# Another written-out order for a convolution and feed-forward kernel: the transposing DMAs of h get a larger latency in the plan

## The chip, the cores and the metric

The kernel runs on one core of a Trainium2 chip. The metric is the device time of one execution in microseconds, the median of nine runs. A core has five engines that each follow an instruction queue of their own in order: the matrix engine (PE), the vector engine (DVE), the scalar engine (ACT), GpSimd (POOL) and SP, which here does nothing but issue DMAs. An instruction waits on semaphores for what it needs from other queues, and everything behind it in its queue waits with it.

## The reference

Four layers work on x of 2048 rows by 512 columns in bfloat16: a gated long convolution, a SwiGLU feed-forward layer, and the same two again with the same weights.

```python
def _A_ref(q, k, v, shift_k, ssm_k, ssm_D):
    # k_shift: a causal filter of 4 taps per column over k
    kv = k_shift * v
    # y[s] = sum over t <= s of ssm_k[:, s - t] * kv[t], by FFTs of length 2 * 2048
    y = y + kv * ssm_D[None, None, :]
    return q * y

def _B_ref(x, w_gate, w_up, w_down):
    g = _silu(x @ w_gate)
    u = x @ w_up
    return (g * u) @ w_down

x = A_q
x = x + _A_ref(_layernorm(x, axis=-1), A_k, A_v, A_shift_k, A_ssm_k, A_ssm_D)
x = x + _B_ref(_layernorm(x, axis=-1), B_w_gate, B_w_up, B_w_down)
x = x + _A_ref(_layernorm(x, axis=-1), A_k, A_v, A_shift_k, A_ssm_k, A_ssm_D)
x = x + _B_ref(_layernorm(x, axis=-1), B_w_gate, B_w_up, B_w_down)
return x
```

The convolution's inputs k, v and ssm_k are the same in both layers, so its result y is computed once and used twice.

## The kernel before

**Tiling.** The 2048 positions are cut into four blocks of 512, and a block into four rows (r = 0 to 3) of 128 positions, one on each partition. The long convolution is done block by block with short Fourier transforms. For block b the filter's values h (the tile `hn`, loaded with columns on the partitions) are turned so that positions lie on the partitions (`hs`), transformed by matmuls with a table (`fwd`), moved out of PSUM by ACT and combined by additions on DVE (`H`, `G`). The same is done with k times v (`vt`, `X`). Products of the spectra are added up in `Z` on DVE (L641 to L655), and matmuls with `inv` give the block of y (`Yk`).

**Turning h.** For blocks 0 and 1, h is transposed on PE (L465). For blocks 2 and 3 `transpose_h_dma` does it (L575 to L585): four copies on ACT (L579) bring `hn` into `hr`, one for each 128 columns, and then SP issues four transposing DMAs (L583), one for each row r, from `hr` to `hs`. A row needs all four copies. The matmuls `ps<-hs,fwd` (L299) use one row each, two per row.

**Feed-forward layer.** It works in units of 256 positions (layer, block c, half h). `prologue` normalises the rows, multiplies with y, adds to x (`xc`), normalises again into `z`, and an SP transposing DMA turns each `z` into `zT` (L831). `ffn` then goes through 14 column blocks of 128 in groups of 4, 4, 4 and 2. Eight matmuls of 256 columns fill one PSUM bank with two blocks of the gate or of the up product (`pf`, L299), ACT applies SiLU (L900, `sg`) or casts (L904, `ht`), DVE multiplies them (L907), and the `pd` matmuls with `wd_sb` (L920) take the product down. The result is added to x by ACT and DVE (L946 to L959), or by a matmul with the identity (L879). PSUM banks come in three rings: `pf` (4), `pd` (2) and `pc` (2).

**What sets the order.** All work is first recorded as a list of operations by `add`, each with its engine, a cost and, for DMAs, a latency. `ORDER` is a table written out in the source with one rank for each of the 1564 operations. `Plan.order` sorts the operations by rank, walks through them with the costs and latencies to choose which buffer of its ring each tile takes, and `Plan.issue` emits them. The instructions of one engine follow each other in that order. Costs and latencies don't move any instruction when `ORDER` is given. They only take part in the choice of buffers, and in the number of warm-up matmuls (L1159) that fill gaps at the start.

**The start.** POOL makes the constants `m` (L974), `eps` (L972), `fq` (L976) and the identity, DVE makes phases from them (L1012, L1016), and ACT makes the Fourier table from the phases by a sine (L1018). DVE clears `drow` (L973), SP loads one row into it (L1003), and DVE adds it to row 0 of h (L478). SP's first nine loads are h, k, the taps, drow, v and x of block 0, h and v of block 1, and the gate weights; two transposing DMAs then turn `fwd` into `inv` (L1069). k of block 0 is transposed on PE (L354, `pt<-ident,kn`), and its taps are applied by matmuls `ps<-dg,kTb`. The first block's y goes straight into the first unit: `m` (L729), `ps<-m,inv` (L735), `n` and `xc` (L837 to L842), `z` (L802), a transpose of z on PE (L854, `ptz`) and two copies into `zT` (L857, L859), after which the first `pf` matmul can run.

Of the kernel before, what the change touches and what calls it, by code (L numbers as in the profile page):

```python
# [48 lines left out]
ORDER = [4, 0, 1, 8, 3, 5, 6, 2, 7, 11, 15, 17, 22, 13, 14, 12, 10, 16, 19, 23, 20, 18, 21, 24, 29, 26, 36, 27, 32, 37, 31, 43, 25, 39, 28, 33, 30,  # L49
         34, 56, 76, 66, 71, 52, 59, 48, 75, 35, 42, 41, 53, 57, 62, 67, 69, 65, 50, 46, 60, 55, 9, 38, 45, 40, 49, 51, 54, 44, 64, 81, 47, 108, 143,  # L50
         148, 154, 63, 70, 77, 78, 83, 73, 74, 80, 82, 87, 84, 89, 90, 93, 96, 61, 68, 85, 88, 92, 86, 79, 91, 98, 94, 103, 105, 121, 127, 135, 173,
         100, 102, 95, 101, 106, 97, 104, 109, 99, 112, 58, 72, 107, 115, 110, 117, 123, 126, 116, 119, 124, 113, 125, 129, 122, 128, 132, 130, 133,
         139, 145, 147, 153, 138, 140, 149, 111, 114, 120, 118, 131, 134, 144, 141, 137, 146, 163, 165, 160, 156, 168, 171, 136, 142, 155, 161, 151,
         157, 162, 170, 158, 166, 152, 177, 198, 200, 167, 188, 194, 207, 174, 181, 172, 150, 178, 179, 191, 218, 164, 185, 176, 190, 175, 180, 182,
         183, 186, 189, 227, 232, 195, 203, 192, 241, 212, 187, 196, 193, 201, 202, 197, 208, 205, 209, 211, 215, 221, 224, 230, 219, 222, 229, 225,
         235, 239, 242, 248, 251, 255, 266, 268, 269, 275, 280, 284, 287, 294, 291, 295, 298, 300, 306, 308, 313, 315, 319, 233, 238, 245, 250, 254,
         247, 262, 257, 199, 206, 216, 204, 217, 223, 169, 184, 213, 214, 220, 226, 270, 277, 282, 285, 293, 303, 234, 237, 243, 279, 288, 292, 231,
         260, 310, 317, 321, 325, 343, 328, 335, 331, 159, 332, 323, 336, 276, 267, 299, 314, 338, 346, 353, 360, 383, 390, 395, 402, 405, 409, 416,
         423, 429, 444, 441, 434, 458, 492, 473, 477, 484, 495, 457, 466, 470, 489, 501, 514, 527, 536, 210, 228, 240, 256, 258, 263, 244, 252, 236,
         246, 273, 302, 283, 253, 264, 249, 259, 261, 272, 278, 286, 307, 316, 311, 271, 301, 289, 297, 274, 290, 296, 304, 309, 320, 324, 305, 312,  # L60
         265, 281, 318, 322, 327, 326, 330, 347, 352, 342, 349, 339, 350, 329, 340, 355, 363, 380, 333, 345, 356, 364, 361, 368, 354, 370, 379, 392,
         396, 371, 384, 367, 373, 375, 382, 351, 366, 387, 404, 400, 385, 394, 388, 397, 401, 406, 403, 408, 410, 413, 334, 337, 341, 344, 348, 357,
         358, 359, 362, 365, 369, 372, 376, 374, 377, 378, 381, 386, 389, 393, 391, 398, 426, 432, 420, 433, 437, 440, 448, 450, 452, 455, 461, 467,
         464, 468, 469, 472, 485, 491, 480, 482, 422, 425, 407, 415, 424, 428, 411, 417, 438, 462, 475, 414, 419, 451, 471, 418, 430, 436, 460, 476,
         488, 493, 446, 454, 431, 439, 427, 445, 465, 474, 481, 500, 497, 479, 487, 443, 490, 494, 503, 506, 524, 516, 551, 622, 675, 399, 435, 447,
         456, 478, 483, 486, 509, 499, 510, 512, 521, 523, 518, 525, 533, 537, 548, 559, 546, 550, 496, 507, 504, 532, 535, 543, 557, 555, 560, 564,
         568, 583, 570, 579, 588, 592, 613, 617, 600, 604, 412, 421, 449, 442, 453, 459, 498, 502, 554, 558, 566, 571, 505, 534, 545, 549, 553, 565,
         575, 578, 539, 541, 526, 530, 590, 584, 603, 606, 595, 597, 609, 616, 585, 625, 593, 463, 601, 589, 581, 610, 632, 620, 596, 634, 608, 615,
         643, 640, 633, 645, 654, 660, 666, 680, 670, 687, 709, 698, 702, 713, 717, 692, 695, 699, 710, 731, 736, 724, 727, 719, 722, 725, 732, 741,
         745, 761, 751, 757, 754, 708, 626, 684, 734, 629, 624, 637, 649, 662, 672, 678, 682, 766, 773, 778, 781, 786, 791, 801, 811, 822, 817, 848,  # L70
         845, 864, 859, 855, 863, 874, 881, 858, 872, 877, 916, 869, 875, 886, 899, 915, 927, 937, 934, 946, 952, 964, 960, 973, 986, 513, 519, 511,
         515, 517, 522, 508, 538, 542, 572, 586, 540, 573, 556, 563, 531, 552, 528, 544, 576, 614, 598, 520, 529, 567, 574, 562, 569, 547, 561, 580,
         623, 628, 577, 587, 591, 599, 621, 641, 644, 661, 651, 676, 679, 691, 631, 639, 594, 605, 611, 618, 619, 630, 642, 671, 664, 648, 653, 582,
         612, 635, 647, 602, 636, 658, 677, 674, 659, 665, 638, 655, 646, 650, 652, 657, 668, 681, 685, 656, 663, 607, 627, 669, 683, 688, 686, 690,
         693, 667, 673, 689, 697, 706, 715, 694, 704, 723, 755, 733, 714, 729, 720, 749, 737, 743, 701, 712, 763, 769, 772, 759, 765, 747, 752, 750,
         762, 726, 738, 770, 777, 775, 764, 774, 742, 748, 776, 780, 779, 784, 782, 790, 700, 705, 696, 703, 707, 711, 716, 718, 721, 728, 730, 739,
         735, 740, 744, 746, 753, 756, 760, 758, 767, 795, 799, 797, 800, 806, 809, 816, 820, 819, 826, 829, 834, 838, 832, 837, 839, 843, 851, 860,
         865, 853, 857, 813, 802, 783, 788, 798, 804, 792, 796, 789, 793, 808, 835, 824, 794, 805, 803, 810, 821, 830, 818, 823, 841, 850, 846, 787,
         812, 814, 825, 807, 815, 842, 847, 852, 861, 866, 828, 856, 831, 836, 862, 873, 871, 876, 892, 888, 910, 771, 768, 785, 827, 833, 844, 849,
         868, 880, 890, 896, 904, 909, 906, 912, 914, 917, 926, 945, 949, 938, 943, 882, 895, 854, 894, 913, 923, 951, 965, 953, 969, 978, 989, 985,  # L80
         993, 995, 1007, 1011, 1014, 1025, 1029, 1027, 1034, 867, 870, 840, 878, 903, 883, 891, 898, 954, 959, 961, 975, 974, 977, 931, 956, 966,
         970, 925, 930, 919, 921, 939, 941, 982, 991, 996, 1004, 999, 1002, 1018, 1012, 1031, 1060, 972, 1064, 1038, 1000, 1054, 983, 1026, 1020,
         924, 1033, 1057, 1081, 1045, 1078, 1066, 1075, 1088, 1096, 1108, 1114, 1101, 1133, 1138, 1139, 1143, 1140, 1145, 1165, 1170, 1163, 1168,
         1147, 1150, 1151, 1154, 1174, 1179, 1156, 1158, 1183, 1188, 1201, 1193, 1196, 1198, 1061, 1030, 1035, 1040, 1056, 1062, 1051, 1094, 1141,
         1210, 1205, 1226, 1231, 1240, 1236, 1243, 1248, 1253, 1258, 1263, 1273, 1265, 1267, 1268, 1272, 1275, 1278, 1289, 1305, 1288, 1291, 893,
         900, 879, 885, 902, 907, 884, 889, 922, 935, 944, 911, 929, 887, 901, 920, 933, 897, 908, 942, 955, 962, 928, 947, 932, 936, 905, 918, 940,
         950, 957, 971, 988, 958, 963, 948, 968, 981, 998, 1008, 1013, 1021, 1044, 1050, 1048, 967, 979, 976, 987, 980, 997, 990, 1006, 1009, 1019,
         1039, 994, 1003, 1005, 1017, 1001, 1015, 984, 992, 1022, 1036, 1042, 1032, 1041, 1028, 1037, 1010, 1043, 1016, 1024, 1047, 1063, 1055, 1046,
         1053, 1023, 1049, 1059, 1067, 1065, 1070, 1068, 1073, 1120, 1083, 1072, 1077, 1058, 1071, 1076, 1089, 1079, 1091, 1100, 1121, 1115, 1052,
         1085, 1099, 1106, 1084, 1092, 1103, 1110, 1113, 1127, 1132, 1112, 1119, 1090, 1098, 1095, 1104, 1069, 1074, 1125, 1135, 1144, 1109, 1117,  # L90
         1128, 1134, 1136, 1142, 1148, 1146, 1153, 1080, 1086, 1082, 1087, 1093, 1097, 1105, 1102, 1107, 1111, 1116, 1122, 1118, 1123, 1124, 1126,
         1130, 1137, 1129, 1131, 1149, 1159, 1155, 1160, 1161, 1164, 1171, 1172, 1175, 1178, 1186, 1182, 1189, 1197, 1192, 1200, 1204, 1217, 1225,
         1215, 1218, 1169, 1177, 1152, 1162, 1167, 1173, 1157, 1166, 1181, 1191, 1207, 1199, 1206, 1194, 1208, 1180, 1190, 1184, 1212, 1219, 1224,
         1232, 1176, 1185, 1203, 1209, 1187, 1195, 1211, 1216, 1222, 1229, 1238, 1214, 1223, 1221, 1227, 1230, 1235, 1241, 1254, 1262, 1270, 1360,
# [141 lines left out]
def kernel(  # L236
# [18 lines left out]
    KD, NF = D // P, F // P  # L255
# [319 lines left out]
    def transpose_h_dma(b):  # L575
        hr = new("s8", "hr", [P, R, KD, P], parts=KD)
        hs = new("hs", "hs", [P, R, D], parts=R)
        for dt in range(KD):
            add("ACT", 0.565, lambda dt=dt: nc.scalar.copy(  # L579
                out=hr.t[:, :, dt], in_=hn[b].t[:, dt, :].rearrange("d (p r) -> d r p", r=R)), r=[hn[b]], w=[(hr, (dt,))],  # L580
                conv=True)
# [611 lines left out]
```

## Time and profile before

| | |
|---|---|
| median of nine runs | 347.36 us (346.83 to 349.63) |
| profiled execution | 347.36 us |
| its span, first to last instruction | 345.6 us |
| granted clock of PE | 1.00 |
| PE busy | 336.7 us, 97% |
| DVE busy | 279.0 us, 81% |
| ACT busy | 253.8 us, 73% |
| DMAs | 22.96 MB, 66 GB/s on average |

The profile is one execution. Its time stands above its span by what lies around the first and the last instruction. A busy share is the union of an engine's instructions, and it is an average over stages: DVE is busier in the first two thirds than in the last. A wait is the idle time in front of an instruction, together with the instruction or DMA that ended it. A transposing DMA has two durations: how long SP is occupied with issuing it, and how long it takes from issue until its last part has landed. Matmuls overlap: each takes longer than the distance between the starts of two, so lengths of work on PE are counted from start to start.

### The profile page before, as it was taken

How to read it: one execution, taken by the hardware profiler on the slowest of the kernel's cores; microseconds unless marked ns; L12 is line 12 of the kernel's file. 1: busy time of each engine (PE TensorE's matmuls, PEld its weight loads, DVE VectorE, ACT ScalarE, POOL GpSimd, SP SyncE). 2: the span in 40 equal slices, each digit the busy share in tenths (PEclk: the TensorE clock that was granted, in tenths of full speed). 3: DMA queues.
4: the chain of work that ended last, by engine and by line, in shares of the span. 5: the costliest groups of instructions: out<-in, count | busy, mean ns of one | idle time of the engine just before them, and what ended most of it. 6: DMA issues, size and time to landing. Idle time of an engine off the chain costs nothing.

```text
span 345.6 us, 6549 instructions
## 1 busy us (share of the span) xinstructions
PE 336.7 (97%) x2577; PEld 248.3 (72%) x2611; DVE 279.0 (81%) x472; ACT 253.8 (73%) x503; POOL 40.7 (12%) x46
## 2 busy tenths in 40 slices
PE   7999999999999999999989999999999999999996
PEld 6656867777687767777576777767685877777783
DVE  6899999999999997999999999969997424636021
ACT  5999998759499957949878999569684544546361
POOL 3200012103121001101220010200201000001000
PEclk9999999999999999999999999999999999999999
DMA  7998007001410336300231012310201110010101
GB/s 278 332 289 285 2 15 201 15 17 30 63 32 17 91 74 157 85 8 2 41 86 30 2 30 93 61 32 1 32 0 34 30 32 0 17 30 12 20 32 46
DMA packets 42089, 22.96 MB, mean 66 GB/s; under 512 B 33861, under 2 KB 39882, under 8 KB 42058
## 3 DMA queue, kind: packets, MB, share of 16 engines
q1 hardware_dynamic: 41914, 22.48, 25.2%
q8 instruction: 20, 0.33, 0.4%
q14 instruction: 11, 0.09, 0.1%
q10 hardware_dynamic: 144, 0.07, 0.1%
HBM read 12.33 MB, written 2.10 MB: 42 GB/s over the span
## 4 chain that ended last, share of the span: by engine, by line
PE 88%; DMA 5%; SPq 3%; DVE 2%; issue 1%; ACT 0%; POOL 0%
PE pf L299 55%; PE pd L920 28%; PE ps L299 4%; DMA wd_sb<-in_B_w_down_dram 2%; SPq L1069 2%; DMA hs<-hr 1%; DMA hn<-in_A_ssm_k_dram 1%; SPq L342 1%; PE pt L465 0%; SPq L583 0%; DVE bnst L747 0%; DVE kTb L362 0%; DVE dg L1051 0%; DVE xc L842 0%; PE pd L879 0%
## 5 line engine op out<-in xcount | busy, mean ns | idle before, releaser
L299 PE MATMUL pf<-zT,wu_sb 128*128 128x256 bf16 x896 | 112.0, 273 | 0.2
L299 PE MATMUL pf<-zT,wg_sb 128*128 128x256 bf16 x896 | 110.2, 273 | 0.2
L920 PE MATMUL pd<-wd_sb,ht 128*128 128x512 bf16 (+1 forms) x438 | 101.7, 372 | 1.2
L299 PEld LDWEIGHTS <-wu_sb 128*128 128x128 bf16 x896 | 87.7, 98 | 18.9
L299 PEld LDWEIGHTS <-wg_sb 128*128 128x128 bf16 x896 | 87.7, 98 | 17.3 <-issue 1.2
L904 ACT CAST ht<-pf 128x512 bf16<-128x512 f32 x112 | 64.5, 592 | 28.5 <-PE pf L299 28.1
L900 ACT ACTIVATE sg<-pf 128x512 bf16<-128x512 f32 x112 | 66.0, 600 | 23.8 <-PE pf L299 19.9
L920 PEld LDWEIGHTS <-ht 128*128 128x128 bf16 x462 | 45.1, 98 | 41.8 <-DVE ht L907 0.3
L907 DVE TENSOR_TENSOR ht<-ht,sg 128x1024 bf16<-128x1024 bf16 (+1 forms) x64 | 39.1, 621 | 21.9 <-ACT ht L904 15.4
L752 POOL TENSOR_TENSOR rstd<-ve,nhalf 128x2 f32<-128x2 f32 x24 | 26.5, 1107 | 216.5 <-DVE ve L750 216.5
L747 DVE BATCH_NORM_STATS2 bnst<-xc 128x6 f32<-128x512 bf16 x48 | 31.5, 685 | 1.8 <-ACT xc L946 1.3
L956 ACT CAST dn<-pd 128x512 bf16<-128x512 f32 x24 | 13.7, 592 | 19.0 <-PE pd L920 19.0
L959 DVE TENSOR_TENSOR xc<-xc,dn 128x1024 bf16<-128x1024 bf16 x12 | 8.3, 689 | 19.5 <-ACT dn L956 19.5
L641 DVE TENSOR_TENSOR t<-X,G 128x2048 bf16<-128x2048 bf16 x18 | 22.0, 1220 | 0.0
L645 DVE TENSOR_TENSOR t<-X,G 128x2048 bf16<-128x2048 bf16 x18 | 21.9, 1218 | 0.1
L407 ACT ACTIVATE X<-ps 128x512 bf16<-128x512 f32 x32 | 18.5, 604 | 3.2 <-PE ps L299 2.9
L778 POOL TENSOR_TENSOR rstd<-ve,nhalf 128x2 f32<-128x2 f32 x8 | 10.0, 1248 | 54.4 <-ACT ve L776 54.4
L407 ACT ACTIVATE H<-ps 128x512 bf16<-128x512 f32 x24 | 14.2, 623 | 1.4 <-PE ps L299 1.3
L655 DVE TENSOR_TENSOR Z<-Z,t 128x2048 bf16<-128x2048 bf16 x12 | 14.7, 1222 | 0.1
L653 DVE TENSOR_TENSOR t<-t,t 128x2048 bf16<-128x2048 bf16 x12 | 14.6, 1218 | 0.1
L299 PE MATMUL ps<-hs,fwd 128*128 128x512 bf16 x39 | 12.8, 379 | 1.6 <-DMA hs<-hr 1.0
L592 ACT ACTIVATE ka<-kTb,tapF 128x512 bf16<-128x512 bf16 x16 | 12.2, 781 | 0.0
(108 smaller groups left out, 322.2 us busy)
## 6 DMA issues: line engine op xcount, KB each, us to landing
hn<-in_A_ssm_k_dram SPq DMA_DIRECT2D x4, 512.0 KB, 5.4
vt<-in_A_v_dram SPq DMA_DIRECT2D x4, 512.0 KB, 4.8
xc<-in_A_q_dram SPq DMA_DIRECT2D x4, 512.0 KB, 5.8
out_dram<-xc SPq DMA_DIRECT2D x15, 128.0 KB, 1.9
wg_sb<-in_B_w_gate_dram SPq DMA_DIRECT2D x1, 1792.0 KB, 12.2
wu_sb<-in_B_w_up_dram SPq DMA_DIRECT2D x1, 1792.0 KB, 7.7
wd_sb<-in_B_w_down_dram SPq DMA_DIRECT2D x1, 1280.0 KB, 13.0
kn<-in_A_k_dram SPq DMA_DIRECT2D x1, 512.0 KB, 4.8
```

The lines of the kernel that those rows point to most:

```text
L299: nc.tensor.matmul(o, lhsT=lhsT, rhs=rhs, start=(n == 0), stop=(n == len(terms) - 1))
L407: add("ACT", act(D), lambda: nc.scalar.activation(out=view(), in_=ps.t[:], func=ACT.Copy, scale=scale), r=[ps], w=[(buf, keys)], conv=conv)
L641: dve(n * D, lambda t1=t1, part=part: nc.vector.tensor_mul(out=t1.t[:], in0=x.t[:, sl, 0, :], in1=g.t[:, sl, part, :]), [(x, key(slots, (0 ...
L645: dve(n * D, lambda t2=t2, part=part: nc.vector.tensor_mul(out=t2.t[:], in0=x.t[:, sl, 1, :], in1=g.t[:, sl, 1 - part, :]), [(x, key(slots ...
L653: dve(n * D, lambda t1=t1, t2=t2, comb=comb: nc.vector.tensor_tensor(out=t1.t[:], in0=t1.t[:], in1=t2.t[:], op=comb), [t2], [t1], conv=conv)
L655: dve(n * D, lambda t1=t1, part=part: nc.vector.tensor_add(out=z.t[:, sl, part, :], in0=z.t[:, sl, part, :], in1=t1.t[:]), [t1], [zk], con ...
L747: add("DVE", 0.6, lambda st=st, i=i: nc.vector.bn_stats(out=st.t[:], in_=xs[c].t[:, i, :]), r=[(xs[c], (i,))], w=[st])
L752: add("POOL", pw, lambda: nc.gpsimd.tensor_tensor(out=rstd.t[:], in0=ve.t[:], in1=nhalf.t[:].to_broadcast((P, n)), op=ALU.pow), r=[ve, nha ...
L900: add("ACT", act(D), lambda ps=ps, o=o, sg=sg: nc.scalar.activation(out=sg.t[:, o:o + 2, :], in_=ps.t[:], func=ACT.Silu), r=[ps], w=[(sg, ...
L904: add("ACT", act(D), lambda ps=ps, o=o, ht=ht: nc.scalar.copy(out=ht.t[:, o:o + 2, :], in_=ps.t[:]), r=[ps], w=[(ht, (o // 2,))], due=(uni ...
L907: dve(n * W, lambda sg=sg, ht=ht: nc.vector.tensor_mul(out=ht.t[:], in0=ht.t[:], in1=sg.t[:]), [sg], [ht], due=(unit, k / pairs, 0.0, "h"))
L920: nc.tensor.matmul((pds[o] if not cs.start else pds[HP]).t[:, cs], lhsT=ht.t[:, q, o * P:(o + 1) * P], rhs=wt["d"].t[:, ft, cs], start=(ft ...
```

## The change

It writes another permutation into `ORDER` and changes two latencies. The list of operations and their costs stay, and with them the number and kind of all instructions, the 24 warm-up matmuls among them.

```diff
-ORDER = [4, 0, 1, 8, 3, 5, 6, 2, 7, 11, 15, 17, 22, 13, 14, 12, 10, 16, 19, 23, 20, 18, 21, 24, 29, 26, 36, 27, 32, 37, 31, 43, 25, 39, 28, 33, 30,
+ORDER = [0, 3, 14, 1, 4, 6, 5, 2, 7, 12, 16, 20, 24, 13, 9, 8, 10, 15, 18, 21, 17, 22, 19, 25, 27, 23, 36, 28, 33, 38, 30, 43, 32, 37, 29, 34, 26,
...
-                out=hs.t[:, r].rearrange("p (k f) -> p k f", k=KD), in_=hr.t[:, r]), r=[hr], w=[(hs, (r,))], lat=3.0 if b == 1 else 1.4, conv=True)
+                out=hs.t[:, r].rearrange("p (k f) -> p k f", k=KD), in_=hr.t[:, r]), r=[hr], w=[(hs, (r,))], lat=3.0 if b == 1 else 1.9, conv=True)
...
-                    out=zT.t[:, :, o, :], in_=z.t[:].rearrange("p (k f) -> p k f", k=KD)), r=[z], w=[(zT, (o,))], lat=1.4)
+                    out=zT.t[:, :, o, :], in_=z.t[:].rearrange("p (k f) -> p k f", k=KD)), r=[z], w=[(zT, (o,))], lat=1.5)
```

The ranks themselves can't be read. What they do to an engine shows when the built instructions are laid side by side. On SP, from the sixteenth DMA on, the first part of the two queues is (xN: N in a row):

```
before                              after
xc<-in_A_q                          xc<-in_A_q
zT<-z x2                            kTb<-in_A_k
kTb<-in_A_k                         hn<-in_A_ssm_k
hn<-in_A_ssm_k                      zT<-z x4
vt<-in_A_v                          hs<-hr x4
zT<-z x2                            hn<-in_A_ssm_k
hs<-hr x2                           zT<-z x2
zT<-z x2                            out<-xc
hs<-hr x2                           zT<-z
zT<-z x4                            out<-xc
out<-xc                             vt<-in_A_v
hn<-in_A_ssm_k                      zT<-z x2
kc<-ka x3                           kc<-ka x3
```

For the second h, the queue before has `hs<-hr`, `out<-xc`, `hs<-hr` x3, `out<-xc`, and the queue after has `hs<-hr` x4 with `zT<-z` on both sides.

On the other engines the same kinds of instructions stand in other places:

- At the start, POOL makes `m` ahead of `eps`, `fq` and the identity, where before it came behind them. DVE clears `drow` behind the first four phases (L1012) instead of ahead of all. On PE the first two `ps<-hs,fwd` matmuls come ahead of the sixteen transposes of k.
- For block 1, whose h PE transposes, ACT's two copies into `hs` (L475) follow each other, where before a few spectra lay between them.
- ACT's copies into `hr` come earlier for both h: by PE's matmuls of the whole program, the last one stands after 20% instead of 23%, and after 45% instead of 49%.
- In the last unit, the last `pf` group stands closer to the end: eight `pd` matmuls of 512 columns and eight of 256 lie between it and the `pd` matmuls that use it.

## The prediction

> **What bounds the kernel now.** First the table of busy shares, then what the matrix engine (PE) waits for, then its timeline at the one place that shows a wait behind the start.
>
> ```profile
> PE 336.7 (97%) x2577; PEld 248.3 (72%) x2611; DVE 279.0 (81%) x472; ACT 253.8 (73%) x503; POOL 40.7 (12%) x46
> ...
> PE wm L1159 <- POOL ident masks.py:199: 1.7, 1, 1.7
> PE ps L299 <- DMA hs<-hr: 1.0, 1, 1.0
> PE ptz L854 <- DVE z L802: 0.4, 1, 0.4
> ```
>
> PE has work in 336.7 of 345.6 us. Behind the start (34 us) its only wait is the second row, 1.0 us for the transposed h. Everything else that PE waits for lies in the first 34 us, and the last 3 us are output copies and their transfers. No instruction is added or removed, so this change can only move waits: PE's matmuls cost the same in any order.
>
> ```profile
> 175.02 2.78 PE L299 MATMUL pf<-zT,wg_sb 128*128 128x256 bf16 x24
> 178.84 0.38 PE L299 MATMUL ps<-hs,fwd 128*128 128x512 bf16 x1 [1.04 <-DMA hs<-hr]
> 179.06 1.03 PE L299 MATMUL pf<-zT,wg_sb 128*128 128x256 bf16 x8
> ```
>
> Columns are start, length, instruction, idle before. Eight pf matmuls start every 0.873 us (0.109 each), so PE could have started the hs matmul at 175.02 + 24 x 0.109 = 177.64. It started at 178.84: 1.20 us lost. That is the length that I use; the 1.04 of the row leaves out the tail of the matmul before.
>
> Why h was late stands in SP's timeline and the view of the tile hs in the same stretch:
>
> ```profile
> 171.16 1.19 SPq L583 DMA_TRANSPOSE hs<-hr  x1
> 172.40 0.58 SPq L967 DMA_DIRECT2D out_dram<-xc  x1
> 173.02 5.06 SPq L583 DMA_TRANSPOSE hs<-hr  x3
> 178.19 0.51 SPq L967 DMA_DIRECT2D out_dram<-xc  x1
> ...
> DMA to landing us min/median/max: 2.4/2.9/4.2
> ```
>
> Four transposes leave SP at 171.16, 173.02, 174.57 and 176.27. The first hs matmul needs row 3, which is the third; the chain of waits gives it 4.24 us to land (174.56 to 178.81), against 2.4 for the quickest.
>
> **A rule against this change.** The Trainium skill, DMA: Bandwidth & Descriptors, section Anatomy of one DMA, puts a transfer at some 2.0 us fixed plus its bytes at 436 GB/s (fitted there on GpSimd's path). For 128 KB that is an estimate of 2.3 us: the third transpose would land at 176.9, ahead of 177.64, there would be no stall to take away and the time would stay at 347.4. The row has 4.24 and PE's wait ends with it, so the row decides: there are 1.20 us to win, and no more anywhere behind the start.
>
> **The change part by part.**
>
> The two latencies (1.4 to 1.9, 1.4 to 1.5) emit nothing. At build they reach only the choice of buffers: 0.
>
> *The transposes of h.* I laid the changed order's instructions side by side and added PE's matmuls between an instruction and its user (0.216 us for 512 columns, 0.109 for 256, 0.056 for 128). Before, 7.2 us of PE work lie between the last copy into hr and the first hs matmul of the stalled h. Afterwards it is 15.9 us for that h and 8.0 us for the other (10.9 before). What counts is which of the four SP issues comes first to use: afterwards both h begin with the row that SP issues first; the fourth-issued row has 18.7 and 13.4 us. Even the stalled run of four took only 171.16 to 179.2, 8.0 us, and a first row takes 2.4. In the trace the hr copy ended some 0.8 us behind its place in PE's order. The least margin is 8.0 - 0.8 - 2.4 = 4.8 us. The stall goes: -1.20.
>
> *SP's queue, which issues in order.* Two loads (kTb and hn of h 2) move ahead of the first zT transposes, and a vt load behind several of them. hs now goes out four together, with no output write between. Loads keep at least 13 us of PE work between issue and use behind the start. A zT transpose needs 1.2 for a predecessor plus 2.4 (row: issue 1.20, landing 2.4); the shortest cover from normalising to the pf matmul is 3.9 us before, and no wait shows there; afterwards it is 4.7. Cost 0. Without that cover a zT transpose as late as the slow hs one would cost 0.6: its last part came 1.72 after the other fifteen (4.24 for 2.52), less the 1.1 that the cover has to spare.
>
> *PE, ACT and DVE behind 34 us.* For PSUM the shortest time between a bank's last matmul and its next use is 1.09 us in both orders (six places before, four after), and the six show no wait. From a pf group to the pd matmuls the shortest is 1.73 before, without a wait, and 2.59 after. DVE is the engine to watch:
>
> ```profile
> core 0: us, PE busy (x) PEld busy (x) DVE busy (x) ACT busy (x) POOL busy (x), PEclk, DMA share, GB/s
> 34.00:70.00 36.00, 35.79 (x275) 27.03 (x277) 35.05 (x50) 31.26 (x69) 5.11 (x4) 1.00 0.23 58
> 70.00:104.00 34.00, 33.90 (x259) 25.49 (x261) 32.93 (x59) 25.33 (x52) 7.13 (x5) 1.00 0.20 34
> ```
>
> Up to 171 us it is busy over 95% beside a full PE. Adding its durations by the order, 1.8 us more of its work now stands in the second stretch (34.1 for 32.3), 1.7 less in the one behind it. The queue that this piles up peaks at 3.1 us of work, against 3.2 at its worst place before, which showed no wait. I take 0; if the cover is short, it is the rival below.
>
> *The start.* POOL makes m ahead of ident, so ident and PE's warm-up come 0.13 us later (the iota's row). DVE clears drow behind four ph instructions; SP's load of drow waits for that clear, at about 2.5 us for 2.19, and vt and x are queued behind it, some 0.4 us later. vt lands about 7.7 with its first use at 11.7, x about 9.1 with its use at 11.3: hidden, 0.4 if they were not. Two hs matmuls go ahead of the kn transposes, filled by rows copied at 6.0 and 6.3. From 14 to 33 us DVE runs almost without a gap towards z, and the first pf matmul (34.07) follows the copy of zT that ends at 33.77. The same DVE instructions stand ahead of z in both orders, so both arrive alike: +0.05, between -0.2 and +0.5 (the last if the two h copies that ACT now makes in a row hold up X's last slot).
>
> *A second rule, on the warm-up.* The row of the first sixteen transposes is 4.78, 1.70 long: 0.107 apart, against 0.056 later. TensorE: Matmul & The Clock Gate, What's actually happening, says that full clock follows a busy window of about 3.4 us and that the window runs freely. If 0.13 us of delay missed a window's start, half clock would last 3.4 us more: +1.7 at most by the rule. By the row, full clock comes 4.6 us after the first warm-up matmul, which leaves 1.2 us of possible starts; 0.13 of that is a tenth of the runs. A median takes 0.
>
> *The end.* The last pf group is now 2.6 us of matmuls ahead of its pd; it needs two ACT evacuations (0.48 + 0.60), one DVE product (0.42) and hand-overs of some 0.45 in all: 1.95. Cost 0; 0.6 if SiLU behind the cast runs late.
>
> Sum against the profiled execution: span 345.6, with 1.76 around it 347.36, which is also the median of the nine. 347.36 - 1.20 + 0.05 = 346.21, **346.2 us**.
>
> **The rivals.**
>
> *The stall is given back.* A DMA as late as 4.24 hits a zT transpose instead, whose cover is 4.7 or more, or the start loses 0.5. For: such lateness is a matter of what else the rings carry. Against: thirty zT transposes before have a median landing of 2.4 and no wait. One such event costs 0.5 to 1.2: 346.7 to 347.4.
>
> *DVE becomes the bound (slower).* Place: PE's stretch of 66 to 100 us of work, where 34.1 us of DVE work face 34 of PE. If the pile of 3.1 us meets a product that the pd matmuls want with only 2.6 us of cover, every later product is late too, PE stops on its PSUM banks, and ACT behind them. It decides the sign once PE loses 2.24 us (the 1.20 won and 1.04 more), for which the pile would have to exceed its cover by that: some 7% on DVE's 34 us. For: shares over 95%. Against: the products there have 4.6 us or more, and a like pile before cost nothing. Time 348.4 to 350.
>
> *The change does nothing:* the stall stays although the cover grew. Only if hr itself were copied 5 us late, and ACT has gaps in every stretch: 347.4, folded into the first rival.
>
> **How the numbers follow.** A measurement of this kernel tells 0.3% (1.04 us) from no change: under 346.32 is faster. The forecast has 0.64; its own range is 345.7 to 346.7, and the border runs through it: 0.50 below, 0.14 above. The stall given back has 0.14, all within. DVE as the bound has 0.22. Faster 0.50, same 0.28, slower 0.22. The range 345.6 to 349.0 leaves out half of the slow rival and a little below.
>
> **What would show it.** PE's waits behind 34 us without hs<-hr; hs issued as four in a row, its first matmul long after the landing; PE's busy time unchanged and the idle 1 us less; the first pf matmul within 0.3 of 34.07. Wrong, if the first pf comes over half a microsecond later, or if PE waits for ht, zT or a PSUM bank anywhere behind it.

## The result and the profile after

The changed kernel takes 345.94 us, the median of ten runs (345.42 to 346.51). The kernel before, run beside it, has a median of 347.40 us (31 runs, 346.74 to 350.46). The ratio is 0.995, with an interval of 0.9932 to 0.9968: faster by 0.5%, or 1.46 us by the medians. The forecast was 346.2.

The profiled execution of the changed kernel is not a usual one. It took 348.15 us, longer than each of the ten, because its first 36 us ran late; a second profile of the same kernel took 346.51. What lies behind the start is alike in both, and is read first. Three views of the first profile: the busy shares, PE's waits over the whole span, and PE's timeline at the second h.

```profile
PE 338.9 (98%) x2578; PEld 249.4 (72%) x2611; DVE 279.1 (81%) x472; ACT 252.6 (73%) x503; POOL 44.2 (13%) x46
```

```profile
PE wm L1159 <- POOL ident masks.py:199: 1.7, 1, 1.7
PE pt L1045 <- DMA tapR<-in_A_shift_k_dram: 0.5, 1, 0.5
```

```profile
172.25 0.59 PE L920 MATMUL pd<-wd_sb,ht 128*128 128x512 bf16 x2
172.68 0.38 PE L299 MATMUL ps<-hs,fwd 128*128 128x512 bf16 x1
172.90 1.04 PE L299 MATMUL pf<-zT,wg_sb 128*128 128x256 bf16 x8
```

The row of 1.0 us for hs is gone from the waits, and so is every other wait behind the start. The first matmul on the second h starts with no idle in front of it. PE's busy sum reads 2.2 us more than before; that is no added work. The matmuls are the same, and more of them ran in the slow clock at the start; in the second profile the sum is 337.8.

SP's timeline and the view of the tile hs in the same stretch:

```profile
157.93 5.83 SPq L583 DMA_TRANSPOSE hs<-hr  x4
168.26 15.86 SPq L831 DMA_TRANSPOSE zT<-z  x4
...
DMA to landing us min/median/max: 2.4/3.1/4.0
```

The four transposes leave SP in a row from 157.93 on, and the first matmul that reads them starts at 172.68. One of the four still lands 4.0 us after issue, as late as the one that cost 1.2 us before. Now nobody waits for it. The DMAs did not become quicker; the wait went because of the lead.

The lead needs ACT as well as SP. Its last copy into `hr` for this h, in the kernel before and in the changed one:

```profile
170.47 0.67 ACT L579 COPY hr<-hn 128x512 bf16<-128x512 bf16 x1
```

```profile
156.67 1.23 ACT L579 COPY hr<-hn 128x512 bf16<-128x512 bf16 x2
```

Before, the copy ends at 171.13 us and the first transpose leaves SP at 171.16; now they are 157.90 and 157.93. In both orders the first of the four goes out as soon as `hr` is complete, so it could not have left earlier before.

The two stretches in which DVE was to be watched:

```profile
34.00:70.00 36.00, 35.75 (x282) 27.20 (x284) 35.20 (x53) 33.57 (x76) 5.58 (x5) 1.00 0.17 35
70.00:104.00 34.00, 33.89 (x250) 24.45 (x250) 32.80 (x60) 27.77 (x57) 9.45 (x5) 1.00 0.27 64
```

DVE (the third pair) has 35.20 and 32.80 us, against 35.05 and 32.93 before, and PE (the first pair) stays full. The second profile has 35.40 and 32.79.

Now the start. PE's timeline in the two profiles of the changed kernel, first the one of 348.15 us, then the one of 346.51:

```profile
4.54 1.86 PE L465 MATMUL pt<-ident,hn 128*128 128x128 bf16 x16
6.90 0.29 PE L1045 MATMUL pt<-ident,tapR 4*128 4x4 bf16 x4 [0.49 <-DMA tapR<-in_A_shift_k_dram]
7.12 1.03 PE L299 MATMUL ps<-hs,fwd 128*128 128x512 bf16 x2
7.95 1.91 PE L354 MATMUL pt<-ident,kn 128*128 128x128 bf16 x16
9.65 1.81 PE L299 MATMUL ps<-hs,fwd 128*128 128x512 bf16 x5
```

```profile
4.54 1.86 PE L465 MATMUL pt<-ident,hn 128*128 128x128 bf16 x16
6.34 0.29 PE L1045 MATMUL pt<-ident,tapR 4*128 4x4 bf16 x4
6.57 1.03 PE L299 MATMUL ps<-hs,fwd 128*128 128x512 bf16 x2
7.39 1.14 PE L354 MATMUL pt<-ident,kn 128*128 128x128 bf16 x16
8.37 1.46 PE L299 MATMUL ps<-hs,fwd 128*128 128x512 bf16 x5
```

Sixteen transposes of k take 1.91 us in one and 1.14 in the other: 0.107 us apart from start to start is the slow clock, 0.056 the full one. In the first profile the trace's record of the granted clock has full speed from 10.4 us on, in the second from 7.5 (before: 6.2), and in the first the load of the taps was 0.5 us late besides. So the same program reaches its first pf matmul at 36.16 us in one execution and at 34.52 in the other. To keep this apart from the change, each run below is read in two parts: the start of the first pf matmul, and the time from there to the start of the last matmul. What follows the last start is 3.2 to 3.4 us in all of them.

| profile | first pf | from it to the last matmul |
|---|---|---|
| before | 34.07 | 308.19 |
| changed | 36.16 | 306.92 |
| changed, second profile | 34.52 | 306.92 |

The second part is the same to 0.01 us in both profiles of the changed kernel, and 1.27 us shorter than before. That is where the gain lies.

### The profile page after: what moved, and what is told of

Read it like the earlier page. It is cut to its first block, busy times and chain, and to the rows that moved or that the text cites. A ratio compares the mean times of both kernels' runs of the same rounds, so it can differ in the third digit from the quotient of the medians.

```text
span 346.4 us, 6541 instructions
## 1 busy us (share of the span) xinstructions
PE 338.9 (98%) x2578; PEld 249.4 (72%) x2611; DVE 279.1 (81%) x472; ACT 252.6 (73%) x503; POOL 44.2 (13%) x46
## 4 chain that ended last, share of the span: by engine, by line
PE 85%; DVE 11%; DMA 1%; issue 1%; POOL 0%; ACT 0%; SPq 0%
PE pf L299 51%; PE pd L920 26%; PE ps L299 6%; DMA tapR<-in_A_shift_k_dram 1%; DVE m L528 1%; DVE t L630 1%; DVE Z L634 1%; PE ps L735 1%; DVE Z L655 1%; DVE t L653 1%; DVE t L641 1%; DVE ht L907 1%; DVE vt L512 1%; DVE m L729 1%; PE pt L354 0%
## 5 line engine op out<-in xcount | busy, mean ns | idle before, releaser
L900 ACT ACTIVATE sg<-pf 128x512 bf16<-128x512 f32 x112 | 64.9, 605 | 16.5 <-PE pf L299 13.0
L907 DVE TENSOR_TENSOR ht<-ht,sg 128x1024 bf16<-128x1024 bf16 x64 | 39.4, 621 | 20.8 <-ACT ht L904 12.4
L752 POOL TENSOR_TENSOR rstd<-ve,nhalf 128x2 f32<-128x2 f32 x24 | 28.8, 1200 | 194.9 <-DVE ve L750 194.9
L778 POOL TENSOR_TENSOR rstd<-ve,nhalf 128x2 f32<-128x2 f32 x8 | 11.4, 1423 | 71.2 <-ACT ve L776 71.2
L824 DVE TENSOR_TENSOR n<-n,Yk 128x1024 bf16<-128x1024 bf16 x15 | 10.3, 690 | 4.5 <-ACT Yk L679 3.5
```

What stands on the lines that cost most here:

```text
L752: add("POOL", pw, lambda: nc.gpsimd.tensor_tensor(out=rstd.t[:], in0=ve.t[:], in1=nhalf.t[:].to_broadcast((P, n)), op=ALU.pow), r=[ve, nha ...
L900: add("ACT", act(D), lambda ps=ps, o=o, sg=sg: nc.scalar.activation(out=sg.t[:, o:o + 2, :], in_=ps.t[:], func=ACT.Silu), r=[ps], w=[(sg, ...
L907: dve(n * W, lambda sg=sg, ht=ht: nc.vector.tensor_mul(out=ht.t[:], in0=ht.t[:], in1=sg.t[:]), [sg], [ht], due=(unit, k / pairs, 0.0, "h"))
```

## The experiments

Ten runs were made. Here are their medians, their ratios to the kernel before (run beside each, medians 347.33 to 347.39), and the two parts of their one profile:

| run | median us | ratio, interval | first pf | from it to the last matmul |
|---|---|---|---|---|
| changed again | 346.00 | 0.9955 (0.9940 to 0.9970) | 34.52 | 306.92 |
| old start, new rest | 346.01 | 0.9959 (0.9945 to 0.9972) | 33.83 | 306.93 |
| new start, old rest | 347.91 | 1.0014 (1.0004 to 1.0025) | 34.06 | 308.90 |
| new order, second h issued late | 347.67 | 1.0013 (1.0002 to 1.0023) | 34.06 | 308.75 |
| before, two matmuls exchanged | 346.59 | 0.9978 (0.9962 to 0.9995) | 34.06 | 307.66 |
| before, 48 narrow warm-ups | 346.81 | 0.9985 (0.9975 to 0.9995) | 33.80 | 307.77 |
| before, 12 wide warm-ups | 347.01 | 0.9992 (0.9983 to 1.0002) | 33.63 | 307.70 |
| before, 80 small warm-ups | 346.65 | 0.9978 (0.9956 to 1.0000) | 35.73 | 307.81 |
| the same, two matmuls exchanged | 346.55 | 0.9977 (0.9962 to 0.9992) | 37.82 | 307.25 |
| changed, earlier warm-up | 345.87 | 0.9959 (0.9944 to 0.9973) | 33.55 | 306.92 |

### Which half of the order earns the time

Two crossed orders: one keeps the order before for the 236 operations up to the first pf matmul and takes the new one behind it, the other the reverse. The first lines of the two tables, against the kernel before:

```diff
 # old start, new rest: the first six lines of ORDER stay, and from the seventh on
-         183, 186, 189, 227, 232, 195, 203, 192, 241, 212, 187, 196, 193, 201, 202, 197, 208, 205, 209, 211, 215, 221, 224, 230, 219, 222, 229, 225,
...
 # new start, old rest
-ORDER = [4, 0, 1, 8, 3, 5, 6, 2, 7, 11, 15, 17, 22, 13, 14, 12, 10, 16, 19, 23, 20, 18, 21, 24, 29, 26, 36, 27, 32, 37, 31, 43, 25, 39, 28, 33, 30,
+ORDER = [0, 3, 14, 1, 4, 6, 5, 2, 7, 12, 16, 20, 24, 13, 9, 8, 10, 15, 18, 21, 17, 22, 19, 25, 27, 23, 36, 28, 33, 38, 30, 43, 32, 37, 29, 34, 26,
...
```

Old start, new rest:

> The order of the kernel before up to the first pf matmul (236 operations), and the changed order behind it. Theory: all of the changed kernel's gain, ratio 0.9955 to 0.997, and in the profile no wait for hs. Rival (the start brings a part of the gain, 0.3 us or more of the 1.5 that the medians show): this kernel stays 0.3 us or more behind the changed one in the same run, 346.3 or above against 345.9.

New start, old rest:

> The changed order up to the first pf matmul and the order of before behind it. Theory: no gain, ratio 0.999 to 1.001 (347.3), and PE's wait for hs of about 1 us is in the profile. Rival (start): ratio 0.999 or below by what the start is worth, 347.0 or less.

The old start with the new rest has all of the gain, 0.9959. The new start with the old rest has none; at 1.0014 it is even 0.5 us slower than before, a little above the 1.001 expected. PE's waits behind 34 us in that run:

```profile
PE ps L299 <- DMA hs<-hr: 1.3, 1, 1.3
```

The old wait is there, and by starts it costs 1.49 us instead of 1.20: the third transpose is again the late one. Smaller losses of 0.19 us near 49 us and 0.29 near 248 make up the rest of its 308.90. Its first pf stands at 34.06, so the new start itself gave nothing and cost nothing.

The changed kernel was also run again:

> The changed kernel itself, for a second profile and for a comparison in the same run with the three others. The profiled execution of it was slow at the start (348.15 us): the matmul distance stayed at 0.107 us up to about 10 us, where the execution of before changed to 0.056 at 6.4. Theory (which execution meets a late full clock is chance): this profile has full clock by 6.5 us, its first pf matmul within 0.3 us of 34.1 and a time of 345.4 to 346.5. Rival (the new order of POOL and DVE at the start makes a late clock the rule): again over 348 us in the profile, with 0.107 up to about 10 us.

Its profile lies between the two: full clock at 7.5 us instead of 6.5, the first pf at 34.52, 0.45 from 34.07 instead of 0.3, and 346.51 us in all. None of its six executions is late (345.25 to 346.56), so a late clock is not the rule in the new order.

### Is it the second h alone?

The changed order, with only the four transposes of the second h moved back behind the zT transpose that they followed before:

```diff
...
-         995, 1002, 1014, 1004, 1021, 1024, 1042, 1044, 1035, 1038, 808, 774, 811, 789, 816, 822, 829, 833, 885, 892, 933, 948, 973, 976, 950, 959,
+         995, 1002, 1014, 1004, 1021, 1024, 1042, 1044, 1035, 1038, 808, 774, 811, 789, 871, 872, 873, 874, 885, 892, 933, 948, 973, 976, 950, 959,
```

> The changed kernel with one thing undone: the four transposing DMAs of the second h-block are issued right behind the transposing DMA of z that they stood behind in the kernel before, not some 10 us earlier; the rest of the new order stays. Theory (the place of these DMAs is what the change earns): TensorE's wait for hs in the middle is back, and with it 1.0 to 2.5 us: about 347.5 us, ratio to before 1.000 to 1.005. Rival (the other moves of the order bring the gain): no wait of over 0.3 us there and 345.9 us, ratio 0.996.

(The other lines only renumber the ranks between.) It takes 347.67 us: the whole gain is gone. The tile hs and PE's waits in that run:

```profile
DMA to landing us min/median/max: 2.5/2.5/2.5
```

```profile
PE ps L299 <- DMA hs<-hr: 1.5, 2, 1.0
```

The wait is back, in two pieces (0.66 and 1.14 us by starts, 1.80 in all, and 308.75 - 306.92 is 1.83). They end with the landing of the first transpose (171.20) and of the fourth (175.19), both within 2.5 us of their issue. (The view has the landings of these two; by its parts in the trace the second took 3.20, but nobody waited for it.) So a late place costs the time even without a late landing: in this order PE asks for the rows earlier than before. Here the copies into `hr` were early and SP alone was late. The reverse, these transposes and copies moved ahead in the order before, was not run.

### Ask for the late row later

In the kernel before, the first hs matmul reads row 3, the third to be issued, and the second reads row 2. Here these two change places:

```diff
-         970, 925, 930, 919, 921, 939, 941, 982, 991, 996, 1004, 999, 1002, 1018, 1012, 1031, 1060, 972, 1064, 1038, 1000, 1054, 983, 1026, 1020,
+         970, 919, 921, 925, 930, 939, 941, 982, 991, 996, 1004, 999, 1002, 1018, 1012, 1031, 1060, 972, 1064, 1038, 1000, 1054, 983, 1026, 1020,
```

> The kernel before with one exchange: the first two matmuls on the second h (and their evacuations on ACT) change places, so that PE asks first for row 2, which SP issued second and which landed at 175.8 in the trace, and 0.216 + 0.873 us later for row 3, the one that landed at 178.81. Theory (the whole gain is the 1.20 us of PE's wait for hs): the wait shrinks from 1.20 to about 0.1, the ratio to the kernel before is 0.9968 (346.3 us), that is as fast as the changed kernel but for 0.3 us. Rival (the gain lies in the start, or in many small places of the order): the ratio stays at 0.999 or above.

The ratio of 0.9978 is less than the 0.9968 that was expected, although the interval takes it in. The view of hs says why:

```profile
PE ps L299 <- DMA hs<-hr: 0.5, 1, 0.5
...
DMA to landing us min/median/max: 2.4/3.4/4.6
```

By starts 0.66 us is still lost, where 0.1 was expected. The third transpose was issued at 174.71 and landed only 4.63 us later, at 179.3; before it landed at 178.81. The expectation had taken the landing time for fixed. It isn't, and so the next question was what makes that one transfer late.

### What makes the third transpose late

The trace of before holds one thing beside the transposes in those microseconds. The DMA view from 176 to 179.5 us (queue, kind, packets, MB, share of the 16 engines):

```profile
q1 hardware_dynamic: 1048, 0.33, 44.6%
q8 instruction: 1, 0.02, 1.9%
q14 instruction: 1, 0.01, 1.0%
```

Two fetches of instructions are under way: 16 KB on q8 at 176.59 us and 8 KB on q14 at 176.90 (times of the packets in the trace). Whose they are, the view does not say. The third transpose was issued at 174.57 and was about to land. Fifteen of its sixteen parts did, 2.51 us after issue; the last took 4.24. Fetches on q8 come about every 17 us. If they are PE's, its count of instructions decides which DMA they meet. That can be shifted without touching any DMA: change the number of warm-up matmuls, but not their length in sum.

```diff
 # 48 narrow
-        for _ in range(n):
-            nc.tensor.matmul(t[:], lhsT=ident.t[:], rhs=ident.t[:], start=True, stop=True)
+        for _ in range(2 * n):
+            nc.tensor.matmul(t[:64, :64], lhsT=ident.t[:, :64], rhs=ident.t[:, :64], start=True, stop=True)
...
 # 12 wide
+        t = psp.tile([P, 2, P], F32, name="wm", tag=f"{ring}{slot}")
+        for _ in range(n // 2):
+            nc.tensor.matmul(t[:], lhsT=ident.t[:], rhs=ident.t[:].unsqueeze(1).to_broadcast([P, 2, P]), start=True, stop=True)
...
 # 80 small
+        for _ in range(80 * n // 24):
+            nc.tensor.matmul(t[:32, :32], lhsT=ident.t[:, :32], rhs=ident.t[:, :32], start=True, stop=True)
```

**48 narrow warm-ups**, fetch moved ahead:

> The kernel before, with its 24 warm-up matmuls of 128 columns replaced by 48 of 64 columns on 64 x 64 of the same tile: the same TensorE time (about 2.6 us), 24 more weight loads and 24 more matmuls in TensorE's program. By the 16 KB that TensorE's instruction fetch brings about every 17 us for some 15 instructions a us, 48 instructions put every later fetch some 3.3 us earlier: the one that was under way during the third transposing DMA of the second h-block (fetch at 176.6 us, DMA issued at 174.57) comes at about 173.3. Theory (the third DMA is late because an instruction fetch falls on it): it lands about 2.5 us after issue instead of 4.24, the wait for hs in the middle falls from 1.0 us to 0.3 or less, and the ratio to before is about 0.997 (346.3 us), if the second DMA, which now meets the fetch, is not what becomes late by more than 2 us. Rival (the lateness belongs to the DMA's place among the others or to something else): wait 1.0 us and ratio 1.000. If narrow warm-ups take longer than the wide ones the start is later by that much, at most 2.6 us, and the profile's first matmul on A_shift's spectrum says by how much.

The fetch moved with PE's count: it came at 172.8 us (173.3 was expected), under the first and the second transpose. Now these are late: 4.66 and 4.05 us (the latter from its parts in the trace). The third is not late to land but late to leave. SP's timeline and the view of hs:

```profile
170.88 1.19 SPq L583 DMA_TRANSPOSE hs<-hr  x1
172.12 0.58 SPq L967 DMA_DIRECT2D out_dram<-xc  x1
172.74 5.96 SPq L583 DMA_TRANSPOSE hs<-hr  x3
...
DMA to landing us min/median/max: 2.5/2.5/4.7
```

SP needs 5.96 us to issue the last three, 5.06 before. PE still waits, 0.80 us by starts instead of 1.20, and the ratio is 0.9985, not 0.997. The expectation had asked for 0.3 or less unless the second became late by more than 2 us; it did not foresee that a late transfer delays the issue of the next. Behind the late first, the issue of the second occupied SP for 2.83 us, where it took 1.50 before.

**12 wide warm-ups**, fetch moved back:

> The kernel before, with its 24 warm-up matmuls of 128 columns replaced by 12 of 256 columns: the same TensorE time, 24 instructions fewer, so that by the same count TensorE's fetches come some 1.6 us later: at about 178.2 us instead of 176.6, behind the landing of the third transposing DMA (174.57 + 2.5 = 177.1). Theory (fetch makes the DMA late): the third lands at about 2.5 us, the wait in the middle is at most 0.3 us, or it moves to the fourth DMA (issued at 176.3, now with the fetch at its end: up to 1 us); ratio 0.997 to 0.999. Rival (the lateness has another cause): wait 1.0 us, ratio 1.000.

The fetch came at 177.75 us, under the fourth transpose, which took 4.06 us. The third landed in time and the wait for hs is gone, but the gain is hardly to be measured (0.9992, with 1 inside the interval). One row of ACT and two of PE show what took its place:

```profile
180.01 0.77 ACT L592 ACTIVATE kc<-kTb,tapF 128x512 bf16<-128x512 bf16 x1 [1.81 <-DMA hs<-hr]
...
181.16 0.59 ACT L407 ACTIVATE H<-ps 128x512 bf16<-128x512 f32 x1
```

```profile
180.46 1.03 PE L920 MATMUL pd<-wd_sb,ht 128*128 128x512 bf16 x4
181.80 0.38 PE L299 MATMUL ps<-hs,fwd 128*128 128x512 bf16 x1 [0.32 <-ACT H L407]
```

ACT writes `kc` into the ring of buffers that also holds `hr` (both carry the name "s8" in the code), so it waits until the fourth transpose has read `hr`: 1.81 us. Its copy of H stands behind that in its queue, and PE waits for the copy. Two losses, 0.48 and 0.25 us by starts, replace the 1.20. The loss moved to the fourth transpose, within the "up to 1 us" that was expected for it, though through ACT. The 1.20 less these 0.73 is 0.47, and the second part (307.70) is 0.49 shorter than before.

**80 small warm-ups**, fetch ahead of all four:

> The kernel before, with its 24 warm-up matmuls replaced by 80 of 32 x 32 x 32[...]: 56 weight loads and 56 matmuls more in TensorE's program, by 15 instructions a us some 7.5 us of shift. TensorE's instruction fetch then comes at about 169.1 us, ahead of all four transposing DMAs of the second h-block (issued at 171.2, 173.0, 174.6 and 176.3), while the DMAs stay where they were. Theory (a fetch under way makes the third DMA late, and the late DMA is most of the wait): all four land at 2.4 to 2.8 us, the wait for hs is at most 0.3 us, no other wait near it takes its place, and the ratio is about 0.997 (346.3 us), lower than with the fetch on the first and second DMA (0.9985) or on the fourth (0.9992). Rival (the DMAs' place alone costs the time, whatever the fetch does): 0.6 to 1.2 us of loss near 178 us stay, ratio 0.998 to 1.000. If small warm-ups bring the full clock later, the first matmul on the transposed block of the feed-forward comes later by that much, up to 2 us.

The fetch came at 173.5 us, not at the 169.1 expected, and took 1.08 us. The first transpose left at 173.65 in this execution, so the fetch was over before any of the four could land. The DMA view from 174 to 181.5 us and the view of hs:

```profile
q1 hardware_dynamic: 2357, 0.69, 42.4%
q14 instruction: 3, 0.02, 1.6%
```

```profile
L583 SPq DMA_TRANSPOSE hs<-hr x4: 1255/1376/1420, 173.7 to 178.8; - x4
...
  ACT kc L592: 0.3, 1
DMA to landing us min/median/max: 2.5/2.5/2.5
```

No fetch for PE is left in the stretch (q8 is missing), all four transposes land in 2.45 to 2.80 us (the view has the landings of three of them; the second, with 2.80, is read from its parts in the trace), PE is not among those who wait, and between 170 and 190 us PE loses nothing but a missing record. The DMAs follow each other as before, the output write between the first two transposes among them, and their issues moved with PE, which began 1.66 us later and lost 0.83 on the way. So the fetch that met the third transpose was the cause of the whole wait of 1.20 us, and the output write was not. The gain, however, is paid for elsewhere: the same shift puts a fetch on a zT transpose at 51 us.

```profile
L831 SPq DMA_TRANSPOSE zT<-z x2: 1196/1728/2259, 51.2 to 52.5; - x2
...
  PE pf L299: 0.7, 1
...
DMA to landing us min/median/max: 3.5/3.8/4.1
```

It lands after 4.07 us, and PE loses 0.83 us by starts. 308.19 - 1.20 + 0.83 = 307.82, and 307.81 is in the table. The start is spread wider too: six of twelve runs take 345.96 to 346.31 and the others 347.00 to 348.64, and the profiled one has the late clock again (full at 10.05 us, first pf at 35.73). The 80 small matmuls start 27 ns apart, and the last of them 0.3 us earlier than the last of the 24; whether that made the clock late was not tried. Its median is therefore no clean measure of this step; the second part is.

**80 small warm-ups and the exchange of two matmuls:**

> As the run with 80 small warm-up matmuls, and besides that the first two matmuls on the second h-block in exchanged places, so that TensorE asks for its third row first and for the late fourth 1.1 us later. Theory (late landing and missing lead add up to the whole loss): with both gone no wait for hs is left, ratio 0.996 (346.0 us), the same as the changed kernel without moving a DMA. Rival (only an earlier issue gives the whole gain, because the DMAs' buffers and queue hold up other work): 0.3 us or more of waits behind the hs stay, ratio 0.997 to 0.999.

No wait for hs is left and the second part is 307.25, close to the 306.92 of the changed kernel; 0.21 of the 0.33 between them is again a zT transpose, at 57 us. The median has 0.9977, not the 0.996 expected, with the spread of the start in it. Nothing behind hs held up other work, as the rival had said; ACT's wait for `kc` is 0.4 us and goes no further.

### A version that beats both?

The changed kernel waits for nothing but the identity matrix at the start. Here its warm-ups read a tile that DVE clears first of all:

```diff
-        for _ in range(n):
-            nc.tensor.matmul(t[:], lhsT=ident.t[:], rhs=ident.t[:], start=True, stop=True)
+        for _ in range(n + 8):
+            nc.tensor.matmul(t[:], lhsT=wz[:], rhs=wz[:], start=True, stop=True)
...
+        nc.vector.memset(wz[:], 0.0)
```

> The changed kernel with its warm-up matmuls on a tile that VectorE clears at the very start, instead of on the identity that POOL has ready at 1.7 us, and 32 of them instead of 24. Theory (the start is bound by TensorE's clock, full only some 4.6 us after the first warm-up): the first warm-up starts about 0.8 us earlier, so does the full clock, the matmuls of the first spectra at half clock become fewer: about 0.3 us less, 345.6 us, ratio to before 0.995. Rival (the start is bound by its DMA landings and VectorE's chain): waits take the place of the gain, 345.9 us, ratio 0.996. If the 8 more warm-ups run into the first real work, up to 0.9 us more: 346.8.

The warm-up starts at 0.97 us instead of 1.75, and in the profile the first pf matmul comes at 33.55, earlier than in any other. The median is 345.87 us, against 345.94 and 346.00: no difference that these runs can tell. The theory's 345.6 did not come, and the ratio is the rival's 0.996. Its five runs stay between 345.32 and 346.19.

## Why the prediction was right

**The bound and the size of the prize.** That PE was full, and that its one wait behind the start was all there was to win, holds: the second part became shorter by 1.27 us, of which 1.20 was forecast. The other 0.07 was not traced. By the medians the gain is 1.46 us against the 1.15 forecast; the interval of the ratio reaches from 1.1 to 2.4 us and so takes in both. The term of the sum that was small is the wait: it was read from one execution, and the other profile with the old rest (new start, old rest) has 1.49 for it. Whether the unprofiled runs of before wait longer than 1.20 on average stays open.

**Why h was late.** Here the reason was only half right. The forecast took 4.24 us as what this place costs and left the cause to what else the rings carry. The cause is one 16 KB fetch of PE's instructions. With the fetch moved ahead, all four transposes landed in 2.45 to 2.80 us and the wait went, with the order of the DMAs unchanged. The rule that was weighed against the row (the Trainium skill, DMA: Bandwidth & Descriptors, Anatomy of one DMA; an estimate of 2.3 us for 128 KB) is close to the 2.43 us that undisturbed transposes show here. It would have been wrong for the forecast, because it has no term for what else uses the DMA engines. The row was the right choice, but for this program's count of instructions only. That this wait stood there to be won was luck of that count; that an earlier issue would take it away was not.

**The margin.** At least 4.8 us of cover was forecast, for the other h, and it measures 4.8: there the first row landed at 78.37 us and the first matmul on it started at 83.16. The transpose that landed at 4.0 us belongs to the second h, whose first matmul came 12.3 us after its row had landed (160.35 to 172.68). So the least margin was not put to the test by a late transfer.

**SP's queue, PSUM, ACT and the tail.** All were costed at nothing, and no wait of PE's shows behind the first pf in the four profiles of the new rest. That the stall would be given back at a zT transpose did not happen in the changed kernel; it did in the run with small warm-ups, in the order before, where it cost 0.83 us. That rival was real, and its price was rightly placed between 0.5 and 1.2 us.

**DVE as the bound.** It did not come. The forecast counted 1.8 us more of DVE's work in the second stretch. The windows have 32.80 for 32.93 us between 70 and 104, and 32.94 for 33.01 between 66 and 100. That count, made from places in the order, does not give the busy time in a stretch of the clock. Why not was not traced; DVE is nearly full there in both orders, and PE never waited.

**The start.** +0.05 was forecast, between -0.2 and +0.5. Four profiles with the new start have the first pf at 34.06, 34.06, 34.52 and 36.16; three with the old one at 33.83, 34.06 and 34.07. By the runs, the new rest has 0.9955 with the new start and 0.9959 with the old: no difference. The 36.16 fits the second rule (the Trainium skill, TensorE: Matmul & The Clock Gate, What's actually happening): slow clock up to 10.4 us instead of 7.5, 2.8 us longer where a missed window would make it 3.4, and 1.64 us more until the first pf where the forecast had 1.7 at most. That a missed window did it is not shown. In the three profiles with full clock at 10 us or later, PE also stood still for a load at the start, for 0.49, 0.66 and 1.24 us, and in no other for more than 0.38; which came of which was not tried. The forecast gave the case a tenth of the runs and a median of zero. One in eighteen executions of the changed kernel is over 347 us, so it didn't touch the median. The warm-up started only 0.08 us later (1.75 for 1.67), not 0.13. Whether that made it likelier can't be told from one; the kernel before has three of 31 at 349.6 us or more, without a trace.

**What was to be seen.** Most of it came: no wait for hs behind 34 us, four transposes in a row, the first matmul long after the landing, and over 1 us less idle time on PE (8.9 us before, 7.5 and 6.9 after). PE's busy time was to stay and rose by 2.2 and 1.1 us, with the slow clock. The first pf was to be within 0.3 us of 34.07 and is 2.1 and 0.45 off in the two profiles of the changed kernel; by the first of them, the forecast's own sign of being wrong was there, in an execution that turned out to be the rare one.

## What to carry to other kernels

A DMA that lands late in one profile may be late because of something that its place has nothing to do with. Before its duration is used as a price, look in the DMA view for what shared the engines in those microseconds, and ask how many instructions more or less would move that. Where a full engine waits for a transfer, give it a lead that covers the worst landing seen in the trace (here 4.7 us), not the median (2.4). In the changed kernel it no longer mattered which transfer was hit.

## What the runs showed of the hardware

Over the twelve profiles, the 552 transposing DMAs from SBUF to SBUF fall into three groups, by what was under way at some moment between issue and landing. The 422 that met no instruction fetch land in 2.43 us in the median and 2.56 at most. The 93 that met a 16 KB fetch on q8 take 3.44 us, 4.66 at most, and 71 of them are over 2.8. The 37 that met only an 8 KB fetch on q14 take 2.54 us, and 13 of them are over 2.8. The fetches on q8 follow PE's count of instructions: 48 instructions more in the warm-up brought one to 172.8 us instead of 176.6, and 24 fewer to 177.75. Why one packet of 16 KB holds up parts of a transfer for 1 to 2 us was not tried.

Adding or removing a few cheap instructions at the start thus took away a wait of 1.2 us in the middle of a kernel of 347 us and made one of 0.83 us elsewhere. A change of 0.2 or 0.3% that alters PE's count of instructions can be this and nothing else.
